# Attention of part A rewritten: scores formed twice in two sweeps, with outputs, dQ, dK and dV summed in PSUM

## The chip, the cores and the metric

The kernel runs on one core of a Trainium2 chip. The metric is the device time of one execution in microseconds, and the medians of several executions are given. The kernel before takes 16264.47 us (median of 4 runs, 16246.73 to 16272.83).

## The reference

The program computes a forward pass and all its gradients. Two attention layers work on the same input `x` (2048 tokens of 576) and are mixed by a gate. Layer A is the one that changes:

```python
def _A_ref(x, wq, wk, wv, wo):       # S = 2048, H = 32 heads, Dh = 18
    q = (x @ wq).reshape(B, S, H, Dh).transpose(0, 2, 1, 3)
    k = x @ wk                        # one key and value head for all
    v = x @ wv
    scores = einsum('bhqd,bkd->bhqk', q, k) * Dh ** (-0.5)
    p = softmax(scores)
    o = einsum('bhqk,bkd->bhqd', p, v)
    return o.transpose(0, 2, 1, 3).reshape(B, S, H * Dh) @ wo
...
g = sigmoid((x * gate_w).sum(-1, keepdims=True))
out = g * _A_ref(x, ...) + (1 - g) * _B_ref(x, ...)   # B: segments with memory, H = 32, Dh = 128
# the result: out and the gradients (vjp with grad_out) of x, the weights, mem0 and gate_w
```

## The kernel before

Part A has a forward, before B, and a backward, after B. Heads are taken four at a time: each has 18 dimensions and one helper row, 19 rows on one of the four 32-row strips of the TensorE array. A call `mm(..., tp=(row, column))` places a small matmul on a strip, so that matmuls on different strips can run at the same time. The forward puts keys on partitions and adds each step's result to a sum in SBUF:

```python
for kt in range(NKB):                         # 8 groups x 4 x 16 = 512 steps
    ...                                       # 2 tiles of 128x1024: scores of 4 heads
    for pr in range(2):
        pexp = sp.tile([P, 2, 512], BF16, name="a_pexp", bufs=4)
        nc.scalar.activation(pexp[:], spss[pr][:], ACT.Exp, scale=SCALEA)
    ...                                       # 4 column strips: values and row sums into pv
    nc.vector.tensor_tensor(out=oacc[:, :], in0=oacc[:, :], in1=pv[:, :], op=ALU.add)
```

The backward puts queries on partitions, forms scores and dP once for all gradients, and therefore has to turn dS for dQ:

```python
for qt in range(NKT16):                       # 512 steps again
    ...                                       # scores, exp, dP, dsn = dP * exp: four tiles of 128x512 each
    dkvp = ps2.tile([P, 512], F32, name="b_dkvp", bufs=1)
    ...                                       # dK products
    nc.vector.tensor_tensor(out=dKTp[:, k0:k0 + 512], in0=dKTp[:, k0:k0 + 512], in1=dkvp[:, :], op=ALU.add)
    ptrs = ps2.tile([P, 4, 4, P], BF16, name="b_ptrs", bufs=1)
    for i in range(4):
        for j in range(4):
            self.tr(ptrs[:, i, j, :], dsn[i][:, j * P:(j + 1) * P], P)    # 16 transposes
    self.evac(dsT[:, :, :, :], ptrs[:, :, :, :])
    ...                                       # dV products and their add; dQ products and their add
```

The softmax here doesn't subtract the row's maximum and nothing guards it: scores larger than these inputs give would overflow.

## Time and profile before

| stage of the kernel before | from, to (us) | length | PE busy | granted clock |
|---|---|---|---|---|
| A forward attention | 167, 1273 | 1106 | 91% | 0.50 |
| B forward | 1388, 6612 | 5224 | 91% | 0.50 |
| B backward | 7126, 10112 | 2986 | 93% | 0.77 |
| A backward attention | 11050, 15915 | 4865 | 90% | 0.51 |

PE is TensorE's matmul stream, PEld its weight loads, DVE VectorE, ACT ScalarE, POOL GpSimd. The granted clock is the share of full speed that TensorE was allowed. The page shows it over the whole span in 40 slices of 406 us each; a digit is tenths of busy time, or tenths of full clock:

```profile
PE   8997999999999999769999999977898898898897
PEclk6555555555555555677777777995555555555556
```

PE is occupied almost everywhere, yet at half clock (a 5) in slices 2 to 16, which are A's and B's forward, and in slices 28 to 39, A's backward. "Busy" therefore does not mean "at full speed".

### The profile page before, as it was taken

How to read it: one execution, taken by the hardware profiler on the slowest of the kernel's cores; microseconds unless marked ns; L12 is line 12 of the kernel's file. 1: busy time of each engine (PE TensorE's matmuls, PEld its weight loads, DVE VectorE, ACT ScalarE, POOL GpSimd, SP SyncE). 2: the span in 40 equal slices, each digit the busy share in tenths (PEclk: the TensorE clock that was granted, in tenths of full speed). 3: DMA queues.
4: the chain of work that ended last, by engine and by line, in shares of the span. 5: the costliest groups of instructions: out<-in, count | busy, mean ns of one | idle time of the engine just before them, and what ended most of it. 6: DMA issues, size and time to landing. Idle time of an engine off the chain costs nothing. (4 is left out here: it accounts for less than half of the span.)

```text
span 16242.6 us, 424152 instructions
## 1 busy us (share of the span) xinstructions
PE 14387.9 (89%) x194891; PEld 8837.7 (54%) x195001; DVE 6081.6 (37%) x8905; ACT 4154.2 (26%) x6200; POOL 1271.0 (8%) x2288
## 2 busy tenths in 40 slices
PE   8997999999999999769999999977898898898897
PEld 3334666666666666558888887333333333333333
DVE  3442333333333333323333333004454454454457
ACT  6882111111111111112222222002333333333330
POOL 0000000000000000111111111241000000000001
PEclk6555555555555555677777777995555555555556
DMA  1002111111111111442222223431000000000001
GB/s 44 9 9 97 37 39 39 39 39 39 39 39 39 38 38 39 144 138 83 85 80 82 83 85 97 135 105 47 13 1 13 13 1 13 13 1 13 7 1 50
DMA packets 473535, 780.13 MB, mean 48 GB/s; under 512 B 223841, under 2 KB 316818, under 8 KB 468866
## 3 DMA queue, kind: packets, MB, share of 16 engines
q1 hardware_dynamic: 357506, 429.32, 8.3%
q0 software_dynamic: 114240, 323.67, 5.8%
q8 instruction: 1524, 24.97, 0.6%
q14 instruction: 265, 2.17, 0.0%
HBM read 407.54 MB, written 345.18 MB: 46 GB/s over the span
## 5 line engine op out<-in xcount | busy, mean ns | idle before, releaser
L98 PEld LDWEIGHTS <-hTs 128*64 128x64 bf16 (+1 forms) x38400 | 1854.8, 150 | 951.9 <-DVE hTs L250 64.9
L1072 ACT ACTIVATE b_pexp<-b_sdA 128x512 bf16<-128x512 f32 x2048 | 1059.3, 609 | 1704.1 <-PE b_dkvp L98 1698.7
L1082 DVE TENSOR_TENSOR b_dsn<-b_sdA,b_pexp 128x512 bf16<-128x512 f32 x2048 | 1296.0, 684 | 290.9 <-PE b_sdA L98 288.9
L103 PE MATMUL b_ptrs<-identB,b_dsn 128*128 128x128 bf16 x8192 | 1245.8, 308 | 0.0
L98 PE MATMUL b_sdA<-b_kaug,b_qaug 19*128 19x256 bf16 x4096 | 1161.7, 401 | 5.4 <-ACT b_dotok L95 5.4
L98 PE MATMUL b_sdA<-b_vaugT,b_doaug 19*128 19x256 bf16 x4096 | 923.2, 395 | 179.2 <-ACT b_pexp L1072 178.3
L309 DVE RECIPROCAL rden<-pbank 64x512 f32<-64x512 f32 x256 | 840.5, 3322 | 482.6 <-PE pbank L98 482.6
L932 ACT ACTIVATE a_pexp<-a_sps 128x1024 bf16<-128x1024 f32 x1024 | 951.9, 1080 | 135.6 <-PE a_sps L98 128.9
L1090 DVE TENSOR_TENSOR b_dKTp<-b_dKTp,b_dkvp 128x512 f32<-128x512 f32 x512 | 351.8, 687 | 1563.7 <-PE b_dkvp L98 1563.7
L98 PE MATMUL pbank<-Wv,hTs 128*64 128x103 bf16 (+3 forms) x12800 | 912.4, 290 | 0.0
L103 PEld LDWEIGHTS <-b_dsn 128*128 128x128 bf16 x8192 | 705.5, 131 | 374.9 <-issue 374.9
L95 ACT COPY b_dsT<-b_ptrs 128x2048 bf16<-128x2048 bf16 x256 | 477.4, 1865 | 1458.5 <-PE b_ptrs L103 1458.5
L98 PE MATMUL b_dkvp<-b_dsn,b_qtokp 128*32 128x171 bf16 (+1 forms) x6144 | 813.7, 335 | 0.0
L98 PE MATMUL pbank<-Wq,hTs 128*64 128x103 bf16 (+1 forms) x10240 | 710.8, 290 | 85.7 <-DVE hTs L250 64.8
L98 PE MATMUL pbank<-Wqk,hTs 64*64 64x102 bf16 (+1 forms) x5120 | 752.8, 291 | 0.0
L98 PEld LDWEIGHTS <-b_qtokp 128*32 128x32 bf16 x6144 | 295.1, 110 | 786.2 <-issue 786.2
L98 PE MATMUL pbank<-Wk,hTs 128*64 128x103 bf16 (+1 forms) x10240 | 711.0, 290 | 0.0
L98 PE MATMUL pbank<-WoT,gTs 128*64 128x103 bf16 (+3 forms) x12800 | 644.6, 227 | 51.6 <-DMA WoT<-st_WoT 51.3
L98 PEld LDWEIGHTS <-b_doaug 19*128 19x128 bf16 x4096 | 220.5, 101 | 704.6 <-issue 704.4
L98 PE MATMUL a_sps<-a_qaugT,a_kaug 19*128 19x256 bf16 x4096 | 585.3, 402 | 1.1 <-ACT a_qtokp L95 1.1
L98 PEld LDWEIGHTS <-gTs 128*64 128x64 bf16 (+1 forms) x12800 | 458.8, 113 | 232.0 <-issue 52.4
L940 DVE TENSOR_TENSOR a_oacc<-a_oacc,a_pv 128x512 f32<-128x512 f32 x512 | 350.9, 685 | 565.0 <-PE a_pv L98 565.0
(409 smaller groups left out, 19900.9 us busy)
## 6 DMA issues: line engine op xcount, KB each, us to landing
st_q<-q SPq DMA_DIRECT2D x64, 512.0 KB
st_k<-k POOLq DMA_DIRECT2D x64, 512.0 KB, 3.0
st_vT<-vT SPq DMA_DIRECT2D x64, 512.0 KB
st_pnT<-pnT SPq DMA_DIRECT2D x64, 512.0 KB
st_oT<-oT POOLq DMA_DIRECT2D x64, 512.0 KB, 4.1
bq<-st_q SPq DMA_DIRECT2D x64, 512.0 KB
bvT<-st_vT SPq DMA_DIRECT2D x64, 512.0 KB
bk<-st_k POOLq DMA_DIRECT2D x64, 512.0 KB, 4.3
```

Of the source, the lines that this page charges most:

```text
L95: nc.scalar.copy(out, in_)
L98: return self.nc.tensor.matmul(out, lhsT, rhs, start=start, stop=stop, tile_position=tp, skip_group_check=True)
L103: return self.nc.tensor.transpose(out, in_, self.identB[b:b + nrows, b:b + nrows], tile_position=tp)
L309: nc.vector.reciprocal(rden[rows, :], den[rows, :])
L932: nc.scalar.activation(pexp[:], spss[pr][:], ACT.Exp, scale=SCALEA)
L940: nc.vector.tensor_tensor(out=oacc[:, :], in0=oacc[:, :], in1=pv[:, :], op=ALU.add)
L1072: nc.scalar.activation(pe[:, :], sN[i][:, :], ACT.Exp, scale=SCALEA)
L1082: nc.vector.tensor_tensor(out=d_[:, :], in0=dps[i][:, :], in1=pexp[i][:, :], op=ALU.mult)
L1090: nc.vector.tensor_tensor(out=dKTp[:, k0:k0 + 512], in0=dKTp[:, k0:k0 + 512], in1=dkvp[:, :], op=ALU.add)
```

## The change

The intent is to have no transposes of dS and no partial sums that leave PSUM in each step. The attention of A now stands wholly before B. A first sweep with keys on partitions gives outputs and dQ; a second sweep with queries on partitions gives dK and dV. Both form scores, exp, dP and their product again. In the first sweep the sums of E (the exp) use weights 64 columns wide (value, key and helper columns together), and the sums of U = E * dP weights 32 columns wide. The core of the diff:

```diff
-    def a_forward_attn(self, sp, psum):
-    def a_backward(self, tc, keep, sp):
...                                              (their bodies, cut)
+    def a_attention(self, keep, sp, pacc, ps):
+        for g in range(8):
+            ...
+            for qb in range(T // 512):
+                acc = [pacc.tile([P, 512], F32, name=f"a_acc{b}", bufs=1) for b in range(2)]
+                for kt in range(NTT):                       # 16 steps
+                    Es, Us = [], []
+                    for pr in range(2):                     # a pair of heads each
+                        s = ps.tile([P, 2, 512], F32, name="a_w", bufs=3)
+                        for j in range(2):
+                            r = srows[2 * pr + j]
+                            self.mm(s[:, j, :], lhsT=self.kaug[r, ks], rhs=qaug[r, qs], tp=(r.start, 0))
+                        d = ps.tile([P, 2, 512], F32, name="a_w", bufs=3)
+                        for j in range(2):
+                            r = srows[2 * pr + j]
+                            self.mm(d[:, j, :], lhsT=self.vaugT[r, ks], rhs=doT[r, qs], tp=(r.start, 0))
+                        ex = sp.tile([P, 2, 512], BF16, name="a_E", bufs=4)
+                        nc.scalar.activation(ex[:], s[:], ACT.Exp, scale=SCALEA)
+                        u = sp.tile([P, 2, 512], BF16, name="a_U", bufs=4)
+                        nc.vector.tensor_tensor(out=u[:], in0=d[:], in1=ex[:], op=ALU.mult)
+                        ...
+                    for pr in range(2):
+                        ev = self.evA if pr == 0 else self.evB
+                        for j in range(2):                  # 64 columns wide
+                            self.mm(acc[pr][64 * j:64 * j + 64, :], lhsT=ev[:, kt, :], rhs=Es[pr][:, j, :],
+                                    start=(kt == 0), stop=False, tp=(0, 64 * j))
+                    for pr in range(2):
+                        for j in range(2):                  # 32 columns wide
+                            b = 64 * j + (32 if pr == 0 else 0)
+                            self.mm(acc[pr][b:b + 32, :], lhsT=self.ku[:, kt, :], rhs=Us[pr][:, j, :],
+                                    start=False, stop=(kt == NTT - 1), tp=(0, b))
+                ...                                         # evacuation, turning, outputs and dQ
+            for kb in range(T // 512):                      # second sweep: queries on partitions
+                ...                                         # same scores, dP, exp, product
+                        for i in range(4):
+                            self.mm(acc[b][32 * i:32 * i + 32, :], lhsT=lt(i), rhs=src[i // 2][:, i % 2, :],
+                                    start=(qt == 0), stop=(qt == NTT - 1), tp=(0, 32 * i))
...                                              (setup, output stage and last dx pass, cut)
```

## The prediction

> **What bounds the kernel now.** I began with the slices of the span, to find stages and clock, then measured each stage over a stretch of time. Columns: stretch, its length, busy us (instructions) of PE, PEld, DVE, ACT, POOL, then granted TensorE clock, DMA share, GB/s.
>
> ```profile
> 167.00:1273.00 1106.00, 1002.83 (x10304) 344.53 (x10304) 473.30 (x575) 964.57 (x1056) 22.62 (x43) 0.50 0.03 9
> 1388.00:6612.00 5224.00, 4771.13 (x66114) 3449.23 (x66114) 1621.93 (x1662) 737.88 (x1280) 262.72 (x382) 0.50 0.11 38
> 7126.00:10112.00 2986.00, 2788.52 (x66368) 2456.05 (x66368) 1040.82 (x1664) 720.22 (x1216) 321.58 (x704) 0.77 0.26 82
> 11050.00:15915.00 4865.00, 4378.58 (x37256) 1863.78 (x37262) 2443.16 (x3931) 1540.20 (x2340) 96.80 (x117) 0.51 0.03 8
> ```
>
> Row 1 is A's forward attention, row 4 its backward, rows 2 and 3 B's forward and backward, which the change leaves alone. The last A forward output leaves at about 1323.5 us, when B's first weight load is issued; the last B epilogue output ends at 10985. So B with its loads is 10985 - 1323.5 = 9662 us, and A is 16242.6 - 9662 = 6581 us: 1323 before B, 5258 after it. Only those 6581 can shrink.
>
> A's forward runs 512 steps of 2.16 us (1106/512), 87% of which ACT is busy: ACT-bound. The backward takes 9.5 us for each of its 512 steps (4865/512). The groups of instructions in the backward, by form (count, busy us, mean ns, idle before):
>
> ```profile
> L1082 DVE TENSOR_TENSOR b_dsn<-b_sdA,b_pexp 128x512 bf16<-128x512 f32 x2048 | 1296.0, 684 | 290.9 <-PE b_sdA L98 288.9 <-ACT b_pexp L1072 1.8
> L103 PE MATMUL b_ptrs<-identB,b_dsn 128*128 128x128 bf16 x8188 | 1245.2, 308 | 0.0
> L1072 ACT ACTIVATE b_pexp<-b_sdA 128x512 bf16<-128x512 f32 x2048 | 1059.3, 609 | 1704.1 <-PE b_dkvp L98 1698.7 <-PE b_sdA L98 5.3
> L95 ACT COPY b_dsT<-b_ptrs 128x2048 bf16<-128x2048 bf16 x255 | 475.6, 1865 | 1454.4 <-PE b_ptrs L103 1454.4
> L93 DVE COPY b_dsT<-b_ptrs 128x2048 bf16<-128x2048 bf16 x256 | 311.6, 1217 | 0.0
> ```
>
> PE is busy 90% at half clock and the others wait for it. Turning dS so that queries become the contraction costs 1245 us of PE and 475.6 + 311.6 us of copies. Partial sums leave PSUM every step too: the dK and dV adds are 351 + 349 us of DVE, dQ's 144.
>
> A forward timeline gives the pitch of tiled matmuls (start, length, work):
>
> ```profile
> 699.59 3.90 ACT L932 ACTIVATE a_pexp<-a_sps 128x1024 bf16<-128x1024 f32 x4
> 700.10 0.61 PE L98 MATMUL a_pv<-a_pexp,a_vaugtok 128*32 128x171 bf16 x10
> 700.65 0.60 PE L98 MATMUL a_sps<-a_qaugT,a_kaug 19*128 19x256 bf16 x4
> 701.18 0.33 PE L98 MATMUL a_pv<-a_pexp,a_vaugtok 128*32 128x171 bf16 x2
> ```
>
> Four 1024-wide exps take 3.90 us, so one per 0.94-0.97 us in a stream though each lasts 1.08. Four K=19 matmuls of 256 columns hold PE 0.53 us (700.65 to 701.18). At half of 2.4 GHz (Part 1 of the clock page below), 256 columns stream in 0.213 us, so the four overlap; the other 0.32 I read as starts staggered by 0.07 us ((0.60-0.39)/3, one matmul lasting 0.39) and about 0.11 us of changeover between the two kinds of matmul.
>
> **What the Trainium skill says.** "TensorE: Matmul & The Clock Gate", Part 3 (Packing small matmuls), says matmuls on different row or column strips run concurrently, four row tiles of N=512 gaining 3.07x; the pitch above agrees in kind. "TensorEngine Tiling (Array Packing)", Key Properties: "Changing tiling mode (not just tile) drains the TensorE"; my 0.11 us between kinds fits. Part 1 of the first page says the clock is at half rate until activity releases it, with nothing between. The forward's 0.50 agrees, with PE 91% busy, so instruction occupancy alone does not release it here; 0.77 in B's backward must be a mix. "PSUM — Partial Sum Buffer", The four PSUM rules, lets matmuls add in place when only the first clears the bank's quadrant: this permits the new sums, but the trace before, whose attention products span one to four matmuls per sum, cannot show sums over 16 steps.
>
> **The change, part by part.** It keeps two sweeps of 512 steps (8 head groups x 4 x 16). Both now form scores, exp, dP and U = exp*dP over 1024 columns in pairs. Removed: all 8192 dS transposes and their 512 copies, 512 forward adds and the per-step dK, dV, dQ adds, together 787 + 351 + 351 + 349 + 144 = 1982 us of DVE and ACT. Also gone are forward's wide reciprocals (107 us). Added: U is formed twice, i.e. 2048 products of 128x1024 instead of 2048 of 128x512; dP matmuls twice.
>
> Per step, new:
> - DVE: a 512-wide product streams at 1296.0/2048 = 0.633 us. Another 512 columns add 0.53 (in setup a 128x1024 cast out of PSUM lasts 1224 ns, a 128x512 one 690). Two products: 2 x 1.165 = 2.33 us.
> - ACT: two exps, 2 x 0.94 = 1.88 us.
> - PE at half clock, 512 columns = 0.427 us: the eight K=19 matmuls in about three bursts 0.60 + 0.74 + 0.60 = 1.94. First sweep: the four M=64 matmuls, two abreast, 2 x 0.427 + 0.07 + 0.11 = 1.03; four M=32 ones in one or two bursts, 0.74 to 1.2. Together 3.7 to 4.2. Second sweep, 4 + 4 of M=32: 1.94 + 0.74 + 0.74 to 1.2 = 3.4 to 3.9. At full clock roughly 2.2.
> - PSUM slots: the two sums take two banks, leaving three 2-bank slots for s0, d0, s1, d1. The next s1 normally waits for a slot until the last U is done, and that U needs this step's second exp: a loop of matmul pair 0.67 + exp 1.06 + product 1.22 + three handoffs of 0.05-0.1 = 3.15 us (2.9 at full clock). M=32 or M=64 matmuls ahead of s1 in PE's order can put 0.5-0.7 onto it.
>
> So neither DVE's 2.33 nor ACT's 1.88 sets a step; PE and the slot loop do, together. At half clock I choose 3.9 us (mean of both sweeps), at full clock 3.2, and weigh them 70:30: 3.7 us. The weight is from density. Multiply-adds per us, counted from shapes: A forward (8 x 256 x 19 x 128 + 12 x 171 x 128 x 32 per 2.16 us) is 6.2 million, B forward about 6.6, both at clock 0.50; B backward about 12, at 0.77. New: first sweep 35.1 million/3.8 us = 9.2 million, second 26.7/3.6 = 7.4: between, nearer the half-speed stages.
>
> Beside the loop: each first-sweep block (32 times) evacuates two accumulators, turns eight 128x128 f32 tiles and copies 1024 columns, borrowing a slot for some 3.5 us and holding the next accumulation about 1 us: 3-4 us, 110. Each second-sweep block holds about 1.3 us: 40. Each group (8) turns three sets of 16 tiles and waits for the small POOL/DVE chain of its last block before the second sweep: about 25 us, 200. The earlier blocks' small operations lie beside some 60 us of sweep.
>
> Attention: 1024 x 3.7 + 350 = 4139 us, for 1106 + 4865 before. Setup: 160 us (before 167: the token-order q projection goes, the dO projection and gate come). Output, dX and dW matmuls with sums in PSUM: 165 (before 50 + 327). Final dx pass, 16 tiles with three buffers: each round of load, two 0.8 us operations and store is about 7 us per three tiles: 40. B stays at 9662.
>
> Sum: 9662 + 160 + 4139 + 165 + 40 = 14166 span; timed runs sit 20 us above the span (16262.93 against 16242.6): 14186, about 14190 us, 12.7% less.
>
> **Rivals.**
> 1. DVE bounds: slots are scheduled well or the clock doubles, and a step falls to 2.4-2.6 us. For: DVE is the largest streaming load besides PE, and forward came within 15% of its ACT floor. Against: that forward had two score tiles over three slots and no product in the chain. Total: 9662 + 365 + 1024 x 2.6 + 350 + 20 = 13060.
> 2. Slots and PE order cost more: engines wait in turn as in the backward, where its step was 9.5 us against 8.55 of PE busy. For: M=32 matmuls wait for U at the head of PE's order, and changeovers drain PE. A step of 4.5 gives 15000.
> 3. B changes speed with its clock (it is 59% of the time). Its instruction mix is the same, so I expect 0.50 and 0.77 again; a few per cent of 5224 would be 100-200 us.
> 4. Work at the end eats the gain: no; before, the whole backward followed B, now only 40 us do.
>
> **Range and chances.** The step dominates: 3.05 to 4.3 us moves 1024 steps by -665 to +615 us, and boundaries and B add about 100: 13500 to 14800. Slower by over 2% (16588) would need steps above 6 us, over two and a half times DVE's load. Faster 0.97, same 0.02, slower 0.01.
>
> **What would show it right or wrong.** Stages: two sweeps of 32 stretches alternating by group, with pitch near 3.9 and 3.5 us; B starting near 4500 us with its stages' lengths and clocks as before. Waits: score matmuls on DVE's U, exps on scores, and PE near 90% at 0.5-0.6. Groups: no transposes of dS; 2048 products of 1.22 us; exps of 1.06. If DVE is 90% busy rival 1 holds; if PE is under 75% busy at half clock with all engines waiting, rival 2. A clock near 1 through attention, a group handoff over 50 us, or B changed by over 100 us would make the sum wrong where I put it.

## The result

The changed kernel takes 14887.24 us (median of 4 runs, 14869.70 to 14893.78), for 16264.47 before. Ratios here are the mean time of one kernel's runs over that of the other's in the same rounds, so not quite the ratio of the medians: 0.9156, 95% interval 0.9143 to 0.9169. It is 8.4% faster, and 87 us above the top of the predicted range.

The main stages after, over stretches of time (columns as in the prediction's first fence):

```profile
157.00:5017.00 4860.00, 4672.69 (x16992) 963.25 (x16987) 2618.41 (x2353) 2169.74 (x2139) 181.15 (x518) 0.51 0.01 2
5017.00:5140.00 123.00, 117.23 (x984) 59.14 (x982) 31.28 (x70) 32.68 (x66) 17.12 (x28) 0.97 0.19 70
5201.00:10424.00 5223.00, 4770.44 (x66112) 3449.16 (x66112) 1622.02 (x1662) 738.98 (x1280) 262.20 (x382) 0.50 0.11 38
10934.00:13978.00 3044.00, 2832.28 (x66368) 2487.28 (x66364) 1041.66 (x1664) 721.34 (x1216) 318.39 (x704) 0.75 0.27 80
```

Row 1 is the new attention: 4860 us where the prediction has 4139. PE is 96% busy (4672.69 / 4860) at clock 0.51, DVE 54%, ACT 45%. Set side by side, with B taken from its first weight load to the last pass:

| term of the sum | predicted | measured | difference |
|---|---|---|---|
| setup | 160 | 157 | -3 |
| attention, 1024 steps with their boundaries | 4139 | 4860 | +721 |
| output, dX, dW | 165 | 123 | -42 |
| B (14848 - 5140) | 9662 | 9708 | +46 |
| last dx pass | 40 | 44 | +4 |
| timed run against the profiled span (14887 - 14892) | 20 | -5 | -25 |
| sum | 14186 | 14887 | +701 |

The whole miss lies in attention. The groups there, without the matmuls of the sums (count, busy us, mean ns of one, idle before):

```profile
L973 DVE TENSOR_TENSOR a_U<-a_w,a_E 128x1024 bf16<-128x1024 f32 x1024 | 1253.1, 1224 | 963.1 <-ACT a_E L971 962.8
L1044 ACT ACTIVATE a_E<-a_w 128x1024 bf16<-128x1024 f32 x1024 | 1049.1, 1025 | 1375.6 <-PE a_w L98 1374.4
L98 PE MATMUL a_w<-a_kaug,a_qaug 19*128 19x512 bf16 x2048 | 901.7, 600 | 4.8 <-ACT a_E L1044 4.1
```

The products last 1224 ns and the exps 1025, close to what was predicted. ACT idles 1374 us before the second sweep's exps, waiting for scores from PE. PE's score matmuls hardly wait at all (4.8 us in the second sweep): PE has more to do in a step than the prediction counted. In the lines below, `a_w<-a_qaug,a_kaug` are score matmuls, `a_w<-a_doT,a_vaugT` dP, `a_acc` the sums; x2 means two matmuls. One step of the first sweep on PE, with the second pair's exp on ACT (start, length, work):

```profile
245.44 0.61 PE L98 MATMUL a_w<-a_qaug,a_kaug 19*128 19x512 bf16 x2
245.84 0.64 PE L98 MATMUL a_w<-a_doT,a_vaugT 19*128 19x512 bf16 x2
...
246.41 0.61 PE L98 MATMUL a_acc<-a_U,a_ku 128*32 128x512 bf16 x2
...
246.95 0.61 PE L98 MATMUL a_w<-a_qaug,a_kaug 19*128 19x512 bf16 x2
...
247.35 0.63 PE L98 MATMUL a_w<-a_doT,a_vaugT 19*128 19x512 bf16 x2
247.60 1.02 ACT L971 ACTIVATE a_E<-a_w 128x1024 bf16<-128x1024 f32 x1 [0.48 <-PE a_w L98]
...
247.91 0.64 PE L98 MATMUL a_acc<-a_E,a_evA 128*64 128x512 bf16 x2
...
248.67 0.64 PE L98 MATMUL a_acc<-a_E,a_evB 128*64 128x512 bf16 x2
...
249.24 0.61 PE L98 MATMUL a_acc<-a_U,a_ku 128*32 128x512 bf16 x2
...
249.78 0.61 PE L98 MATMUL a_w<-a_qaug,a_kaug 19*128 19x512 bf16 x2
```

Read the starts, not the lengths: scores that last 0.61 us are followed on the same strips after 0.40. The step is 4.34 us (245.44 to 249.78), and 404 of the 512 steps of the first sweep are that long. (The 33 steps at 4.67 us, with one score pair split, all lie in the first half of a first sweep's first block; the expectations below were written with 4.67 as the usual step.) The order is not that of the program text: the scheduler that builds the kernel has put 32-wide sums of the step before (246.41) between the two pairs. Each entry is a pair of heads, two of the four strips. The pair's scores and then the pair's dP are 0.40 us apart (245.44 to 245.84): they use the same two strips and go one after the other. I call each such pass a round: 512 columns, 0.427 us at half clock by the reading that the prediction took from "TensorE: Matmul & The Clock Gate", Part 1, and the trace agrees to some hundredths. Where the kind of tile changes, a start follows after 0.54 to 0.57, a round and some 0.11 more. Between the two pairs of 64-wide sums nothing changes, yet 0.76 us pass: the second pair waits for its exp, which ends at 248.62 (247.60 + 1.02).

Counted: 8 rounds, 5 changes of tile and 0.33 us of waiting (0.76 - 0.427): 8 x 0.427 + 5 x 0.11 + 0.33 = 4.30 us, for 4.34 measured. Four abreast wherever possible would be five rounds (scores, dP, two for the 64-wide sums, one for the 32-wide).

In the second sweep a step measured 4.84 us (480.87 to 485.71). Its costly parts are the four dV sums and a score pair that is split:

```profile
481.52 1.02 ACT L1044 ACTIVATE a_E<-a_w 128x1024 bf16<-128x1024 f32 x1 [0.48 <-PE a_w L98]
...
481.84 1.37 PE L98 MATMUL a_acc<-a_E,a_dog 128*32 128x512 bf16 x4
...
483.14 0.60 PE L98 MATMUL a_w<-a_kaug,a_qaug 19*128 19x512 bf16 x1
...
484.21 0.60 PE L98 MATMUL a_w<-a_kaug,a_qaug 19*128 19x512 bf16 x1
484.21 1.02 PE L98 MATMUL a_w<-a_vaugT,a_doaT 19*128 19x512 bf16 x2
...
485.17 0.61 PE L98 MATMUL a_acc<-a_U,a_qtok 128*32 128x512 bf16 x2
```

The dV sums hold PE 1.30 us (481.84 to 483.14), since the second pair of them waits for the exp that ends at 482.54; the last score and two dP need two rounds, 0.96. The same count gives 9 rounds, 6 changes and 0.33 of waiting, 4.83 us. 512 x (4.34 + 4.84) = 4700, so of the stage's 4860 us about 160 lie at the boundaries of blocks and sweeps (the few steps of 4.67 included).

### The profile page after: what moved, and what is told of

Read it like the earlier page. It is cut to its first block, busy times and chain, and to the rows that moved or that the text cites. A ratio compares the mean times of both kernels' runs of the same rounds, so it can differ in the third digit from the quotient of the medians.

```text
span 14892.1 us, 355211 instructions
## 1 busy us (share of the span) xinstructions
PE 13545.5 (91%) x163790; PEld 7557.7 (51%) x163790; DVE 5585.9 (38%) x6393; ACT 3815.3 (26%) x4970; POOL 1269.2 (9%) x2548
## 3 DMA queue, kind: packets, MB, share of 16 engines
q10 hardware_dynamic: 1312, 1.33, 0.0%
## 5 line engine op out<-in xcount | busy, mean ns | idle before, releaser
L1046 DVE TENSOR_TENSOR a_U<-a_w,a_E 128x1024 bf16<-128x1024 f32 x1024 | 1251.7, 1224 | 1131.8 <-ACT a_E L1044 1088.6
L973 DVE TENSOR_TENSOR a_U<-a_w,a_E 128x1024 bf16<-128x1024 f32 x1024 | 1253.1, 1224 | 963.1 <-ACT a_E L971 962.8
L1044 ACT ACTIVATE a_E<-a_w 128x1024 bf16<-128x1024 f32 x1024 | 1049.1, 1025 | 1375.6 <-PE a_w L98 1374.4
L971 ACT ACTIVATE a_E<-a_w 128x1024 bf16<-128x1024 f32 x1024 | 1048.8, 1025 | 1179.5 <-PE a_w L98 1179.5
L98 PE MATMUL a_w<-a_kaug,a_qaug 19*128 19x512 bf16 x2048 | 901.7, 600 | 4.8 <-ACT a_E L1044 4.1
L98 PE MATMUL a_w<-a_vaugT,a_doaT 19*128 19x512 bf16 x2048 | 836.0, 620 | 21.8 <-DVE a_U L1046 15.9
L98 PE MATMUL a_acc<-a_E,a_dog 128*32 128x512 bf16 x2048 | 625.0, 600 | 71.8 <-ACT a_E L1044 0.2
L98 PE MATMUL a_w<-a_doT,a_vaugT 19*128 19x512 bf16 x2048 | 670.8, 623 | 5.2 <-ACT a_E L971 4.1
L98 PE MATMUL a_w<-a_qaug,a_kaug 19*128 19x512 bf16 x2048 | 658.0, 599 | 3.6 <-ACT a_doT L95 3.0
L98 PE MATMUL a_acc<-a_U,a_ku 128*32 128x512 bf16 x2048 | 625.3, 607 | 0.2
L98 PE MATMUL a_acc<-a_U,a_qtok 128*32 128x512 bf16 x2048 | 623.3, 606 | 0.6 <-DVE a_U L1046 0.6
L98 PE MATMUL pkq<-qT,kT 128*64 128x64 bf16 x2048 | 534.3, 261 | 0.0
```

The source lines that it names most:

```text
L98: return self.nc.tensor.matmul(out, lhsT, rhs, start=start, stop=stop, tile_position=tp, skip_group_check=True)
L971: nc.scalar.activation(ex[:], s[:], ACT.Exp, scale=SCALEA)
L973: nc.vector.tensor_tensor(out=u[:], in0=d[:], in1=ex[:], op=ALU.mult)
L1044: nc.scalar.activation(ex[:], s[:], ACT.Exp, scale=SCALEA)
L1046: nc.vector.tensor_tensor(out=u[:], in0=d[:], in1=ex[:], op=ALU.mult)
```

## The experiments

Two questions are asked: why a step is 4.75 us with its share of the boundaries (4860 / 1024), and why the clock stays at half. The first is tried with theories of rounds and order (theory P: PE's rounds and the order in which they come set the step) against the number of rows, the slots and DVE. Unless stated otherwise, a kernel computes the same results and all were correct. The runs of before beside them had medians of 16238.8 to 16253.0 us.

### A step late, and four abreast: lag_order, lag_free, pin_nolag

The sums of a step need its exps and products. In lag_order they are issued one step late, so that PE has more work that is ready, and PE's order is fixed: four scores, four dP, then the previous step's sums. `pin` only adds an ordering dependency between consecutive matmuls, no wait.

```diff
+            def step(sl, sr, dl, dr, ls, rs, sums):
+                for pr in range(2):                        # 4 scores
+                    ...
+                        self.pin(self.mm(s[:, j, :], lhsT=sl[r, ls], rhs=sr[r, rs], tp=(r.start, 0)))
+                for pr in range(2):
+                    ex = sp.tile([P, 2, 512], BF16, name="a_E", bufs=6)
+                    ...
+                for pr in range(2):                        # 4 dP and the products
+                    ...
+                flush()                                    # sums of the step before
+                pend.append(lambda: sums(Es, Us))
```

> Edit: in both sweeps the summing matmuls of a step are emitted one step late, and PE's order is pinned: four score matmuls, four dP matmuls, then the previous step's sums. Same arithmetic. Theory P (PE's order): at half clock PE is the bound of the changed kernel, a step costs 0.427 us for each round of 512 columns that cannot run abreast plus about 0.11 us for each change of tile shape; the changed kernel has 9 rounds and 6-7 changes a step (4.67 and 4.84 us). Here 5 rounds and 3 changes (2.5 us) and 4 rounds and 2 changes (1.9 us), so PE stops being the bound and the loop over three PSUM slots (about 3.15 us) takes over: attention about 1024 x 3.2 + 60 = 3.35 ms instead of 4.86, total 13.2 to 13.6 ms, PE about 75% busy. Rival S (slots): the slot loop already sets the 4.67 and 4.84 and PE's order merely fills it: total within 2% of 14.89 ms. Rival D (DVE): a step cannot fall below 2 x 1.22 us, no objection to P.

lag_free has the same edit with every `self.pin(...)` taken off again, so the scheduler orders PE:

```diff
-                        self.pin(self.mm(s[:, j, :], lhsT=sl[r, ls], rhs=sr[r, rs], tp=(r.start, 0)))
+                        (self.mm(s[:, j, :], lhsT=sl[r, ls], rhs=sr[r, rs], tp=(r.start, 0)))
```

> The same late emission as in lag_order but without pinning, so the scheduler orders PE. Its order splits pairs again: counted from the built program, a first-sweep step is about seven bursts, 8 rounds and 7 changes: 4.2 us; the second sweep similar, 4.2 us. Theory P: attention about 1024 x 4.2 + 50 = 4.35 ms, total about 14.4 ms. Rival S, in which lateness alone removes the wait for this step's products from the loop: the same total as lag_order, 13.4 ms. If the order doesn't matter and nor does lateness: 14.89 ms.

pin_nolag fixes the order and leaves the sums in their own step:

```diff
-                flush()
-                pend.append(lambda: sums(Es, Us))
+                sums(Es, Us)
```

> As lag_order, but each step's sums stand right after its own dP matmuls instead of one step late; PE's order is pinned. Rounds and changes are as few as in lag_order (2.5 and 1.9 us of PE), but now PE waits at the head of its queue: scores 0.6, exp 1.02, two products 2.36, sums of U 0.54, in a row, about 4.7 us in both sweeps. So a good order alone buys nothing: total within 2% of 14.89 ms, with PE under 65% busy in attention. If rounds alone decided (theory P without waits), it would come out like lag_order, 13.76 ms.

Measured, with the changed kernel as the fourth corner (medians, ratio to before):

| | order left to the scheduler | order fixed, four abreast |
|---|---|---|
| sums in their own step | the change: 14887.24 (0.9156) | pin_nolag: 14902.52 (0.9176) |
| sums one step late | lag_free: 14211.87 (0.8735) | lag_order: 13759.28 (0.8468) |

The intervals are 0.9162 to 0.9189 (pin_nolag), 0.8696 to 0.8773 (lag_free) and 0.8450 to 0.8485 (lag_order).

One step of lag_order on PE:

```profile
182.32 0.61 PE L98 MATMUL a_w<-a_qaug,a_kaug 19*128 19x512 bf16 x4
...
182.72 0.63 PE L98 MATMUL a_w<-a_doT,a_vaugT 19*128 19x512 bf16 x2
...
184.04 0.61 PE L98 MATMUL a_w<-a_doT,a_vaugT 19*128 19x512 bf16 x2 [0.69 <-ACT a_E L979]
...
184.58 0.64 PE L98 MATMUL a_acc<-a_E,a_evA 128*64 128x512 bf16 x2
...
185.00 0.64 PE L98 MATMUL a_acc<-a_E,a_evB 128*64 128x512 bf16 x2
185.57 0.62 PE L98 MATMUL a_acc<-a_U,a_ku 128*32 128x512 bf16 x4
...
186.12 0.61 PE L98 MATMUL a_w<-a_qaug,a_kaug 19*128 19x512 bf16 x4
```

Four scores take 0.40 us until the next start (182.32 to 182.72), as two did before, so four strips do run in one round. The step is 3.80 us with six rounds and a wait of 0.69 us for the first exp. The matmuls were never slower one by one; there were fewer rounds. lag_free had a step of 4.27 us in the first sweep with no such wait, and its second sweeps took 242 us for the change's 306. Its median was 1.3% below the 14.4 ms expected; lag_order stands 1.2% above its expected 13.2 to 13.6 ms.

pin_nolag shows that order alone buys nothing:

```profile
202.35 0.61 PE L98 MATMUL a_acc<-a_U,a_ku 128*32 128x512 bf16 x2 [0.25 <-DVE a_U L987]
...
204.61 0.61 PE L98 MATMUL a_w<-a_doT,a_vaugT 19*128 19x512 bf16 x2 [0.69 <-ACT a_E L979]
```

With the sums in their own step PE waits 0.69 us for an exp and 0.25 us for the second product. Its step is 4.65 us in both sweeps (199.96 to 204.61 for the same matmul), where the changed kernel has 4.34 and 4.84. Fewer rounds and longer waits came to the same time as more rounds and shorter waits. Its PE was 77% busy, against my expected under 65%: that number was a miss. All three kernels also name the four scores before the four dP in the program text and keep six buffers of exps and products instead of four. pin_nolag has both and gains nothing; for lag_free no run tells them apart from the lateness.

### Rows: k32

Do more rows cost time? Each strip takes all 32 rows (the 13 added are zero) instead of 19.

```diff
-            srows = [slice(32 * i, 32 * i + 19) for i in range(4)]
+            srows = [slice(32 * i, 32 * i + 32) for i in range(4)]
```

> Edit: the K=19 matmuls of attention use 32 rows a strip instead of 19; the 13 added rows are zeros on both sides, results equal. Rows are free in time, so with the clock as it is the time stays within 0.5% of 14.89 ms. Theory C (PE's clock stays at half because few multiply-adds per us are done: 7.5 and 5.5 million now, 9.0 and 6.9 with 32 rows, if zero rows count; B's backward has 12 at clock 0.77): still below 12, clock stays about 0.5. If the clock rises above 0.6 in attention, strip occupancy is what releases it, and the total falls by 0.5 ms or more.

Measured: 14851.01 us (14844.99 to 14865.93), ratio 0.9144 (0.9130 to 0.9158), which overlaps the change's 0.9143 to 0.9169; attention 4859 us for 4860. A round costs the same with 19 or 32 rows here. As the added rows are zero, this does not test whether more switching in the array would move the clock.

### Sums leave PSUM again: evac_each, lag_evac

evac_each undoes one part of the change: the second sweep's sums leave PSUM in each step, as before.

```diff
-                acc = [pacc.tile([P, 512], F32, name=f"a_acc{b}", bufs=1) for b in range(2)]
                 for qt in range(NTT):
+                    acc = [pacc.tile([P, 512], F32, name=f"a_acc{b}", bufs=1) for b in range(2)]
...
-                                    start=(qt == 0), stop=(qt == NTT - 1), tp=(0, 32 * i))
+                                    start=True, stop=True, tp=(0, 32 * i))
...
+                            nc.vector.tensor_tensor(out=dst[:, ks], in0=dst[:, ks], in1=acc[b][:, :], op=ALU.add)
```

> Edit: one part of the change undone, in the second sweep alone: the dK and dV sums leave PSUM after every step by two DVE adds (0.69 us each) instead of every sixteen steps. If keeping sums in PSUM is what pays (DVE work on the path): 512 x 1.37 = +0.7 ms, 15.6 ms. Theory P: DVE has the room (2 x 1.22 + 1.37 = 3.8 us of a 4.84 us step), so no loss; and the built program's PE order comes out better by chance (pairs not split, about 6 to 7 rounds and 6 changes, 3.7 us): second sweep 3.8 to 4.3 us a step, total 14.3 to 14.6 ms.

Measured: 14459.32 us (14453.82 to 14469.13), ratio 0.8902. It does more work and is 428 us faster. In the changed kernel the four dV sums of a second-sweep step last 1.37 us (the line at 481.84 above). In evac_each:

```profile
500.58 0.61 PE L98 MATMUL a_w<-a_kaug,a_qaug 19*128 19x512 bf16 x2
...
502.20 0.71 PE L98 MATMUL a_acc<-a_E,a_dog 128*32 128x512 bf16 x4
502.85 0.61 PE L98 MATMUL a_w<-a_kaug,a_qaug 19*128 19x512 bf16 x2
```

The same four matmuls take 0.71 us there, because the second exp ends within 0.1 us of their start, and no score pair is split. The step is 3.98 us instead of 4.84, and 512 x 0.86 = 440 us, the whole difference. The scheduler came out with a better order, although only the start flags and the adds had been edited. What the edit was meant to measure is hidden under that, so I repeated it on the fixed order of lag_order:

```diff
                     def sums(Es, Us, qt=qt, ks=ks):
...
-                                        start=(qt == 0), stop=(qt == NTT - 1), tp=(0, 32 * i)))
+                                        start=True, stop=True, tp=(0, 32 * i)))
...                                                  (and the two adds to dst in each step)
```

> lag_order with evac_each's edit: the second sweep's sums leave PSUM after every step (two DVE adds, 1.37 us). In evac_each that was faster than the changed kernel, because PE's order was the bound and got better by the way. Here PE has room and DVE would need 2.36 + 1.37 = 3.7 to 3.9 us instead of a 3.25 us step: second sweep +0.5 to +0.7 us a step, total 14.0 to 14.15 ms against 13.76. If sums in PSUM are worth nothing at all: 13.76.

Measured: 13869.05 us (13859.50 to 13878.93), ratio 0.8540 against lag_order's 0.8468: 110 us slower, less than expected; a second-sweep step of 3.46 us instead of 3.25. With the order held, keeping these sums in PSUM is worth about 0.1 ms. The adds mostly fit in DVE's free time.

### A better order: lag_split

lag_order still waits for the exp between the dP pairs. Here the late sums of E go between scores and dP, and those of U after dP.

```diff
+                if pend:
+                    pend[0][0]()                           # sums of E of the step before
                 for pr in range(2):                        # dP and products
...
-                flush()
-                pend.append(lambda: sums(Es, Us))
+                flush()                                    # sums of U of the step before
+                pend.append((lambda: sums(Es, None), lambda: sums(None, Us)))
```

> As lag_order, with the late sums cut in two: the sums of E stand between scores and dP, the sums of U after dP. In lag_order's first sweep (3.81 us a step) PE waits 0.69 us for the first exp before the second dP pair and then has 1.5 us of sums before the next scores; here 0.97 us of sums fill that wait. First sweep about 3.2 us (slot loop), second unchanged 3.25: total 13.35 to 13.55 ms. If the first sweep is bound by something else (DVE or slots at 3.8), it stays at 13.76.

Measured: 13530.50 us (13512.40 to 13539.77), ratio 0.8330 (0.8318 to 0.8343), as expected in total. The parts were not: the first sweep's step was put at 3.2 us and the second's at 3.25, and the two errors partly cancel. It beats both kernels, by 16.7% and by 9%.

```profile
204.02 0.61 PE L98 MATMUL a_w<-a_doT,a_vaugT 19*128 19x512 bf16 x4
...
205.11 0.60 PE L98 MATMUL a_w<-a_qaug,a_kaug 19*128 19x512 bf16 x2
...
206.01 0.61 PE L98 MATMUL a_w<-a_qaug,a_kaug 19*128 19x512 bf16 x2 [0.30 <-DVE a_U L989]
```

dP is now four abreast, and the wait for the exp is gone. What is left is the slot loop that the prediction had named: the second score pair waits 0.30 us for the product that frees its slot in PSUM. Steps are 3.53 us in the first sweep and 3.08 in the second; the prediction's slot loop was 3.15.

### The clock: lag_fill, split_fill4, split_fill8, first_fill4, first_fill2

All kernels so far ran attention at about 0.51 of full clock on average, although PE was up to 99% busy (lag_free). The average hides one exception. lag_free ran most of its very first sweep at full clock and the seven later first sweeps at half:

```profile
240.00:340.00 100.00, 96.45 (x569) 32.72 (x567) 84.47 (x83) 72.25 (x74) 11.12 (x32) 1.00 0.00 1
640.00:740.00 100.00, 100.00 (x378) 20.64 (x376) 56.04 (x53) 48.26 (x49) 5.56 (x16) 0.50 0.00 1
```

From the first to the last matmul of `a_evA` that sweep took 208 us, the others 276; without it lag_free's gain on the change would be about 4.1% instead of 4.5% (an estimate). So the clock can rise here without any filler, and why it rose there and not later is not known. To see whether the array's density holds the clock down, full 128x128 matmuls of 512 columns with nonzero data were put in front of the scores. The scores overwrite them, so results stay right. lag_fill adds two a step to lag_order:

```diff
+                    for j in range(2 if pr == 0 else 0):
+                        self.pin(self.mm(s[:, j, :], lhsT=self.x_sb[:, 0, 0:P], rhs=self.x_sb[:, 1, 0:512]))
```

> lag_order plus two full 128x128x512 matmuls a step, written into the first score tile and overwritten by the scores (results unchanged): they raise the multiply-adds per us in attention from 7 to 11 million to about 13. Theory C (low activity of the array keeps PE at half clock): the clock rises well above 0.5, the first sweep falls to about 3.1 us a step, total 13.1 to 13.5 ms. If the clock stays at 0.5 they only cost: about 1 us a step in the first sweep and 0.85 in the second, total 14.6 to 14.8 ms.

Measured: 14528.93 us (14488.12 to 14562.68), ratio 0.8945. The clock rose only now and then (0.83 between 260 and 390 us, 0.50 between 430 and 660). Matmuls lasted 0.61 us at 182 us and 0.39 us at 2002 us. It is neither of my two outcomes but nearer to the pessimistic one. The next two add four and eight a step to lag_split:

```diff
+                    for j in range(2):                     # split_fill4: ahead of both score pairs
+                        self.pin(self.mm(s[:, j, :], lhsT=self.x_sb[:, 0, 0:P], rhs=self.x_sb[:, 1, 0:512]))
...
+                    for j in range(2):                     # split_fill8: ahead of both dP pairs as well
+                        self.pin(self.mm(d[:, j, :], lhsT=self.x_sb[:, 0, 0:P], rhs=self.x_sb[:, 1, 0:512]))
```

> Question: does a denser array take the tensor clock from half to full in attention? The two-filler kernel was at half clock most of the time and at full clock in bursts (its matmuls lasted 0.61 us at 182 us, 0.39 at 2002 us). This kernel is lag_split with four full 128x128x512 filler matmuls a step, each overwritten by the scores that follow. Theory H (clock stays at half): four fillers add 4 x 0.427 = 1.7 us a step to PE, of which some 0.3 us were idle before, so 13.53 ms + 1024 x 1.4 = about 14.95 ms, attention clock 0.50 to 0.60. Theory F (density releases the clock): nine rounds of 0.213 us and five changes of 0.1 give 2.4 us of PE, below the slot loop of about 2.9, so about 12.9 to 13.2 ms, attention clock above 0.9, matmuls of 0.39 us.

> As split_fill4 with eight fillers a step, ahead of the scores and of the dP matmuls. Theory H: eight fillers add 3.4 us less some 0.3 idle: 13.53 ms + 1024 x 3.1 = about 16.7 ms at clock 0.5. Theory F: thirteen rounds of 0.213 and seven changes of 0.1 give about 3.5 us a step, near lag_split's own 3.47, so about 13.5 to 13.7 ms at a clock above 0.9. If the clock lies between, PE's step is the mix of the two.

Measured: split_fill4 14136.69 us (14082.54 to 14176.17), split_fill8 14996.70 us (14988.46 to 15017.21). Both lie between their two theories. The reason shows in stretches of 100 us. split_fill4, in a first and a second sweep:

```profile
260.00:360.00 100.00, 93.16 (x616) 27.17 (x614) 73.46 (x75) 64.01 (x64) 11.11 (x32) 1.00 0.00 1
460.00:560.00 100.00, 100.00 (x430) 17.05 (x428) 50.87 (x44) 44.95 (x45) 0.00 (x0) 0.50 0.00 0
```

All eight first sweeps ran at clock 1.00 and all eight second sweeps at 0.50; the clock turned where the sweeps do. PE was busier in the slow stretch (100 against 93), so idle time does not explain it. In the first sweep a step was 3.18 us, below lag_split's 3.53 despite the fillers; in the second it was 4.65 instead of 3.08.

split_fill8, twice in a second sweep:

```profile
2160.00:2260.00 100.00, 100.00 (x588) 25.36 (x588) 60.24 (x54) 46.95 (x49) 0.00 (x0) 1.00 0.00 1
2760.00:2860.00 100.00, 100.00 (x338) 16.16 (x338) 35.57 (x30) 28.67 (x28) 0.00 (x0) 0.50 0.00 0
```

The same instruction mix, PE busy without a break, at full clock in one group and at half in the next: here, as in lag_free, both states are possible. Counted from shapes as in the prediction, with 8.4 million multiply-adds per filler, split_fill4's first sweep does (35.1 + 33.5) / 3.18 = 21.6 million a us and keeps the full clock; its second would do 18.8 at an estimated 3.2 us, and lost it. split_fill8 also ran at full clock only through 15 rounds and 10 changes a first-sweep step (4.32 us), not the 13 and seven I had counted, since fillers split score pairs. So its 13.5 ms were out of reach.

Then the fillers are kept in the first sweep alone, four or two a step:

```diff
+                    for j in range(2 if sl is self.kaug else 0):               # first_fill4
+                    for j in range(2 if sl is self.kaug and pr == 0 else 0):   # first_fill2
+                        self.pin(self.mm(s[:, j, :], lhsT=self.x_sb[:, 0, 0:P], rhs=self.x_sb[:, 1, 0:512]))
```

> In split_fill4 the clock was 1.00 in every first sweep (about 3.18 us a step, against lag_split's 3.53) and 0.50 in every second sweep, where the same fillers only cost. This kernel keeps the four fillers in the first sweep alone. Theory D (the density of the work that runs sets the clock, sweep by sweep): first sweeps at 1.00, second sweeps as in lag_split at 0.50 and 3.08 us; 13530 - 512 x 0.35 = about 13350 us (13300 to 13420). Rival (the clock's rise depends on what went before, such as the second sweep's fillers): first sweeps at half clock, 4.9 us a step, about 14.2 ms.

> The same with two fillers a step, in the first sweep alone. Counted from shapes, a step holds 35.1 million multiply-adds of its own and 16.8 million of filler. In split_fill4 sweeps of 21.6 million a us kept the full clock and sweeps of 18.8 million lost it. Here full clock would mean a step of about 2.9 us and 17.9 million a us, below both, so theory D expects the clock to fall back to half for most of the sweep: step up to 4.0 us, 13.6 to 13.8 ms, first-sweep clock 0.5 to 0.7. If it holds the full clock all the same, 13530 - 512 x 0.6 = about 13.2 ms, and my threshold is wrong.

Measured: first_fill4 13499.79 us (13475.15 to 13508.88), ratio 0.8300 (0.8286 to 0.8314); first_fill2 13419.87 us (13404.68 to 13510.10), ratio 0.8268 (0.8239 to 0.8296). In first_fill4 six of the eight first sweeps ran at 1.00, as theory D expected. Two (around 1060 and 2800 us) ran at half clock for most of their length. From the first to the last matmul of `a_evA` they took 300 and 269 us where the six others took 207, together 155 us more, which is the 150 us missing to the expected 13350:

```profile
1060.00:1160.00 100.00, 99.32 (x392) 18.20 (x388) 46.60 (x46) 40.37 (x40) 5.54 (x16) 0.50 0.00 0
```

So 21.6 million a us is not a safe level either. In first_fill2 the clock wandered, 0.51 to 0.84 in 100-us stretches of first sweeps, and its time fell between my two numbers, so my threshold was too simple. Its median is the shortest, but its runs scatter over 105 us, and the gain on lag_split (0.8268 against 0.8330) is under 1%.

## Why the prediction was wrong

**Right.** The direction, setup, the last stages, B with its clocks, the lengths of products and exps, and that DVE and ACT set no step. The transposes of dS are gone, sums over 16 steps in PSUM give correct results, and the 0.11 us for a change of tile was read rightly. The slot loop of 3.15 us is real, but it only showed once PE's order had been mended (3.08 in lag_split).

**The step that failed** is the cost of a step on PE at half clock: "Together 3.7 to 4.2" in the first sweep and "3.4 to 3.9" in the second, taken as 3.9 for both. The steps shown above have, in us:

| term | predicted | first sweep | second sweep |
|---|---|---|---|
| the eight K=19 matmuls | 1.94 | 0.40 + 0.57 + 0.40 + 0.56 = 1.93 | 0.40 + 0.57 + 0.53 + 0.96 = 2.46 |
| sums of E | 1.03 first, 0.74 second | 0.76 + 0.57 = 1.33 | 1.30 |
| sums of U | 0.74 to 1.2 | 0.54 + 0.54 = 1.08 | 0.54 + 0.54 = 1.08 |
| step | 3.9 | 4.34 | 4.84 |

The prediction put three groups of K=19 matmuls at 0.60 to 0.74 us each and had no term for a wait on the step's own exp. In the second sweep there are three groups, but two of them hold two rounds each (0.97 and 0.96), since pairs on the same strips go one after the other. In the first sweep there are two groups of two rounds, and that their 1.93 meets the 1.94 is luck. In both sweeps the second pair of sums of E waits 0.33 us for its exp. The stagger of 0.07 us does not exist: four 512-column matmuls abreast take 0.55 us with a change in lag_order (185.57 to 186.12), hardly longer than the 0.53 that four of 256 columns took in the kernel before. Those were two rounds of 0.213 and a change, not one round and staggered starts: in the trace they start in two pairs, at 700.65 and 700.84. "TensorE: Matmul & The Clock Gate", Part 3 (Packing small matmuls), gives some 4 ns per tile; lag_order agrees (0.61 us for four, 0.60 for one), and I had the page open beside a reading that contradicted it.

**In terms of the sum**, attention missed by +721 us. At half clock I had 3.9 us a step and the mean of the two sweeps is 4.59: 1024 x 0.69 = +706. The 30% of full clock, taken off by the weight, never came: 1024 x 0.2 = +205. The boundaries were put at 350 and cost about 160: -190. The sum is 721. At half clock alone the prediction would have been 14391, within its range, so the size of the step is the larger error, and boundaries put too high hid part of it. The 20 us of timed run over span compared two different executions; a run's own span is 1.7 us below its time (14892.1 and 14893.78).

**The weight of the clock.** The prediction took density as what decides and interpolated between stages. In the attention of the change, at 8.1 and 5.5 million a us (35.1 / 4.34 and 26.7 / 4.84), there is no rise to speak of: 0.51. The filler kernels show that added full matmuls can raise the clock. That multiply-adds per us decide is not shown: lag_free's fast sweep held 1.00 at 12.7 million (35.1 / 2.76), while first_fill4's slow sweeps stood at 0.50 with 13.5 million (68.6 / 5.1). In the traces the clock is at any time 0.5 or 1.0; values between are means over a stretch.

**The rivals.** Rival 2, with its step of 4.5 us and 15000, was nearest in time and right about PE's order. Its mechanism, waiting in turn with PE under 75% busy, happened only in small: 0.33 us a step, for an exp and not for U, with PE 96% busy. It is nearer to what happened in pin_nolag (77%). Rival 1 needed a better schedule; the best here, lag_split, has 71% of DVE (2520 of 3551 us) and is still not bound by it.

**What stays open** is what exactly the clock's control counts. Why two of the eight first sweeps in first_fill4 ran at half clock, and one of the eight in lag_free at full clock, with the same instructions as the others, is not explained.

## What to carry to other kernels

Count small matmuls in rounds: how many passes of the columns PE makes when strips that coincide cannot overlap, plus the changes of tile and the waits at the head of PE's order, taken from the order that the trace shows and not from the program text. Issue sums that need another engine's result one step late and fix PE's order, so that four strips are filled and nothing waits; doing only one of the two gave 0 and 4.5% here, both 7.6%. Do not credit a full clock because PE is busy, and read the clock per stage.

## What the Trainium skill lacked or had wrong

- "TensorE: Matmul & The Clock Gate", Part 1 (and "HAM oscillation"), ties the full clock to recent PE activity and has a rule of no idle gaps over some 3.4 us. Here PE without a break was at 0.50 (split_fill8, 2760 to 2860 us, 100 of 100 us busy) and at 1.00 with the same mix (2160 to 2260). The change's attention stayed at 0.51 with PE 96% busy. The page lacks that small tiles can leave the clock at half with PE busy without a break (lag_free, 640 to 740 us, 100 of 100 us), that the same tiles can also hold the full clock (lag_free, 240 to 340 us), and that added full 128x128 matmuls can raise it.
- "TensorEngine Tiling (Array Packing)", Key Properties, says that a change of mode drains the array but gives no figure: about 0.11 us at half clock (0.54 less a round of 0.427) and about as much at full clock (0.33 less 0.213 in split_fill4, 179.72 to 180.05).
